# A fused attention and maxout kernel: the maxima of four quadrants go over a scratch row in DRAM instead of a selection product

## The chip, the cores and the metric

The kernel runs on one core of a Trainium2 chip. The metric is the device time of one execution in microseconds; the kernel before took 822.51 us (median of 3 runs, 822.45 to 826.05). A difference of about 0.5% is what a measurement of this kernel can tell from none.

Engines, as the profile names them: PE is TensorE's matmul, PEld its weight load, DVE VectorE, ACT ScalarE, POOL GpSimd, SP the sync engine, which here issues nearly all DMAs from one queue, in order (SPq).

## What is computed

Shapes: x is 4 x 12544 x 128 in float32, 32 inducing vectors of 128, weights 128 x 768 (three of them) and 768 x 128.

```python
def mab(q, kv):
    s = scale * (q @ kv.transpose(0, 2, 1))
    s = s - s.max(-1, keepdims=True)
    a = np.exp(s)
    a /= a.sum(-1, keepdims=True) + 1e-09
    return a @ kv
h = mab(I, x)              # 32 inducing vectors attend over 12544 tokens
x = mab(x, h)              # 12544 tokens attend over 32 states
h = np.maximum(np.maximum(x @ w1, x @ w2), x @ w3)
return h @ w_out
```

The first `mab` is called the first attention here, the second the second attention.

## The kernel before

**Tiling.** The 98 token tiles of a batch (128 tokens each) form seven groups: group 0 has 2 tiles, groups 1 to 6 have 16 each. A full group gives four chunks of 512 columns, group 0 one of 256: 25 chunks a batch, 100 in all. A chunk has six steps j, one for each 128 rows of the hidden width, so there are 600 **slots**.

**One slot** (`advance` and `stage2`): PE makes a product `pu` (line 669) for the next slot into one of two alternating banks and `pv` (675) for this one into another pair; ACT takes the relu of `pu` to `ru` (684); DVE takes the maximum of `pv` and `ru` to `h` (702); ACT rounds `h` to `hi` (691); POOL, or DVE at a few fixed steps, makes the remainder `lo` (699, 705). Six slots later PE adds three products with `hi` and `lo` to `acc` (727 to 729). At the end of a chunk ACT copies `acc` to `o` (744) and SP writes it out (745). Since the `pu` and `pv` banks alternate, a product waits until `ru` or `h` of two slots earlier has been read.

**Windows.** The 24 slots in which the four chunks of a full group g of batch b run are called window g of batch b here; slot numbers below count from the window's first slot (`s0` in the code). In the same window other work is interleaved by hand: the softmax of the second attention for group g + 1 of batch b (`scores_steps`: an exponential, a small sum, `ph` and `pl`), and in batches 0 to 2 the first attention of batch n = b + 1. Window 1 handles groups 0 and 1 of batch n, windows 2 and 3 the groups 2 and 3, window 4 the groups 4 and 5, window 5 group 6. So the first attention of batch 1 runs during batch 0, and so on; that of batch 0 runs before all slots, with code of its own. The matrix products of this work stand in a **burst** at slot 2, and in some windows another at slot 15.

**The order** of every engine is fixed by the program (`manual_schedule`): `plan[s]` holds the steps that `at(s, ...)` and `softmax1`, `softmax2` put into slot s, and `main` runs them after that slot's `advance`.

**A group of the first attention** (`softmax1`). The scores of 32 inducing vectors lie in 128 partitions as four quadrants, each with a quarter of the group's tokens. `attend_max` (line 292) reduces each partition to its negative maximum `mq`. The maximum of a vector is then the least of four partitions, 32 apart:

- `attend_column` (299): ACT multiplies a 128 x 4 mask `quad` by `mq`, giving `md`.
- `attend_spread` (306): PE multiplies `md` by the selection matrix `sel`, so that all 128 partitions hold the four values of their vector in PSUM; in float32 this is two passes, each with a weight load.
- `attend_least` (312, 315, 316): DVE reduces the four values and, from the second group on, takes the least with the running value of the group before.
- `attend_weights` (322): ACT makes the exponential `a` with that value as bias; `attend_scale` (365) makes the factor `al` for the earlier sums; `attend_transpose` (336) transposes `a` on DVE, and `attend_sums` (346) multiplies it with the tokens in a later burst.

The first steps stand at slots s + 2 and s + 3, the others at s + 6 to s + 10, with `LATE` = 12 more slots in windows 2 and 3 (s is 2 or 15).

**Loads.** `load_channels` fetches the transposed tokens xT (1 MB, line 111), `load_tokens` the tokens xg (1 MB, line 100), both on SP's queue, as are the `pT` copies (four per chunk, line 654, from `ph` and `pl`), which are issued two chunks ahead at the fifth slot of each chunk.

Of the kernel before, what the change touches and what calls it, by code (L numbers as in the profile page):

```python
# [8 lines left out]
F32 = mybir.dt.float32  # L9
# [4 lines left out]
ALU = mybir.AluOpType  # L14
AX = mybir.AxisListType
# [10 lines left out]
def kernel(ctx, tc, x, xt, ind_t, w1, w2, w3, w_out, out):  # L26
    nc = tc.nc
    B, N, C = x.shape
    M = ind_t.shape[1]
    DF = w1.shape[1]  # L30
    P = 128
    NT = N // P
    NJ = DF // P
    NQ = P // M
# [18 lines left out]
    ORDER = "a a a a b a a b 0 c d m b a b a b a p d b 1 c s b b b s S m b q 2 c s 3 c s d s s d s"  # L53
    STEPS2 = (3, 5, 7, 8, 9, 10, 11, 13, 14, 15)
    scale = 1.0 / float(C) ** 0.5
    LATE = 12
    LOWVEC = (23, 0, 15, 18)
    LOWLAST = (23, 0, 9, 15, 18)
    UW = 2 * DF + C
# [5 lines left out]
    while t0 < NT:  # L65
        nt = NT % GT if t0 == 0 and NT % GT else GT
        assert nt == GT or nt <= NQ
        g = dict(t0=t0, nt=nt, at=t0 * P)
        groups.append(g)
        t0 += nt  # L70
    NG = len(groups)

    const = ctx.enter_context(tc.tile_pool(name="const", bufs=1))
# [3 lines left out]
    bp = ctx.enter_context(tc.tile_pool(name="bp", bufs=2))  # L77
    hp = ctx.enter_context(tc.tile_pool(name="hp"))
    op = ctx.enter_context(tc.tile_pool(name="op", bufs=2))
    ps = ctx.enter_context(tc.tile_pool(name="ps", bufs=1, space=PSUM))  # L80


# [155 lines left out]
    state = {}  # L238

    def start_batch(b):  # L240
        st = state[b] = {"xT": {}, "xg": {}, "a": {}, "s": {}}
        st["mneg"] = bp.tile([P, NG], F32, name="mneg", tag="mneg")
        st["lst"] = bp.tile([P, NG], F32, name="lst", tag="lst")
        if b == 0:
            st["hg"] = const.tile([P, NG, C], F32, name="hg")
        else:
            st["hs"] = bp.tile([P, C], F32, name="hs", tag="hs")
# [60 lines left out]
    def attend_least(b, gi):  # L308
        st = state[b]
        new, mp = st["mneg"][:, gi : gi + 1], st["mp"]  # L310
        if b == 0 or gi == 0:
            nc.vector.tensor_reduce(out=new, in_=mp[:, :NQ], axis=AX.X, op=ALU.min)
        else:

            nc.vector.tensor_reduce(out=mp[:, NQ : NQ + 1], in_=mp[:, :NQ], axis=AX.X, op=ALU.min)
            nc.vector.tensor_tensor(out=new, in0=mp[:, NQ : NQ + 1], in1=st["mneg"][:, gi - 1 : gi], op=ALU.min)

    def attend_weights(b, gi):
        w = groups[gi]["nt"] * M
        st = state[b]  # L320
        a = wk.tile([P, 512], F32, name="a", tag="a")
        nc.scalar.activation(
            out=a[:, :w],
            in_=st["a"][gi][:, :w],
            func=AF.Exp,
            bias=st["mneg"][:, gi : gi + 1],
            accum_out=st["lst"][:, gi : gi + 1],
        )
        st["a"][gi] = a
# [32 lines left out]
    def attend_scale(b, gi):  # L362
        st = state[b]
        st["al"] = wk.tile([P, 1], F32, name="al", tag="al")
        nc.scalar.activation(
            out=st["al"],
            in_=st["mneg"][:, gi - 1 : gi],
            func=AF.Exp,
            bias=st["mneg"][:, gi : gi + 1],
            scale=-1.0,  # L370
        )

# [397 lines left out]
    def at(s, f, *args):  # L770
        plan[s].append((f, args))
# [13 lines left out]
    def softmax1(b, gi, s, wait=0):  # L785

        at(s + 2, attend_max, b, gi)
        at(s + 3, attend_column, b)
        at(s + 6 + wait, attend_spread, b)
        at(s + 7 + wait, attend_least, b, gi)  # L790
        at(s + 8 + wait, attend_weights, b, gi)
        if gi > 0:
            at(s + 9 + wait, attend_scale, b, gi)
        at(s + 10 + wait, attend_transpose, b, gi)
# [6 lines left out]
    for b in range(B):  # L801
        base = b * per_batch + short
        n = b + 1
        for g in range(1, NG):
# [11 lines left out]
            if n < B:  # L816

                if g == 1:
                    if n == 1:
                        at(s0 + 1, load_tokens, 1, 4)  # L820
                    at(s0 + 4, load_channels, n, 2)
                    first.append((attend_products, n, 0, bank_a[1]))
                    softmax1(n, 0, s0 + 2)
                    second += [(attend_products, n, 1, bank_a[1]), (attend_sums, n, 0)]
                    at(s0 + 16, attend_add, n, 0)
                    softmax1(n, 1, s0 + 15)
                    at(s0 + 16, load_tokens, n + 1, 0)
                    at(s0 + 20, load_channels, n, 3)
                elif g < NG - 2:
                    first += [(attend_products, n, g, bank_a[1]), (attend_sums, n, g - 1)]  # L830
                    at(s0 + 3, attend_add, n, g - 1)
                    softmax1(n, g, s0 + 2, 0 if g == NG - 3 else LATE)
                    at(s0 + 4, load_channels, n, g + 2)
                    more = g + 3
                    if more < NG:
                        at(s0 + 5, load_tokens, n, more)
                    else:
                        at(s0 + 5, load_tokens, n + 1, more - NG + 1)
                    if g == NG - 3:
                        second += [(attend_products, n, g + 1, bank_a[1]), (attend_sums, n, g)]  # L840
                        at(s0 + 16, attend_add, n, g)
                        softmax1(n, g + 1, s0 + 15)
                        at(s0 + 16, load_tokens, n + 1, 2)
                elif g == NG - 2:
                    first += [(attend_products, n, g + 1, bank_a[1]), (attend_sums, n, g)]
                    at(s0 + 3, attend_add, n, g)
                    softmax1(n, g + 1, s0 + 2)
                    at(s0 + 5, load_tokens, n + 1, 3)
                    second.append((attend_sums, n, g + 1))
                    at(s0 + 16, load_tokens, n + 1, 4)  # L850
                    at(s0 + 16, attend_add, n, g + 1)
                    at(s0 + 18, add_quadrants, ("state", n), bank_a[1])
                    at(s0 + 18, total_sums, ("state", n), bank_a[0])
                    at(s0 + 19, invert_total, ("state", n))
                    at(s0 + 19, combine_states, ("state", n), 1)
                    at(s0 + 21, combine_products, ("state", n), bank_a[0])
                    at(s0 + 22, combine_high, ("state", n))
                    at(s0 + 23, combine_low, ("state", n))
                    for r in range(NQ):
                        at(s0 + 25 + 3 * r, combine_rows, ("state", n), r)  # L860
                else:
                    first += [(scores_products, n, 1, bank_a[0]), (scores_products, n, 0, bank_a[1])]
                    softmax2(n, 1, *(s0 + i for i in STEPS2))
                    softmax2(n, 0, *(s0 + i for i in (4, 6, 8, 9, 10, 11, 12, 13, 14, 15)))
                    if n + 1 < B:
                        at(s0 + 18, start_batch, n + 1)
                        at(s0 + 18, load_channels, n + 1, 0)
                        at(s0 + 18, load_channels, n + 1, 1)
# [119 lines left out]
```

## Time and profile before

| What | Before |
|---|---|
| median of 3 runs | 822.51 us |
| span of the profiled execution | 821.3 us |
| median less this span | 1.2 us |
| granted TensorE clock | full in all 40 slices of the page |
| busy: PE, ACT, POOL, DVE | 98%, 91%, 79%, 76% |
| HBM read, written | 48.12 MB, 25.69 MB |
| windows 2, 3 of batch 1 (from the first product of one to that of the next) | 31.3 us each |
| windows 4, 5 of batch 1 | 33.7 and 34.2 us |
| window 2 of batch 3, without a first attention | 28.2 us |

The profile is of one execution. Rows of the timeline give the start, the duration, the engine, the line, the operation, what it writes and reads (output<-inputs) and its shape; in square brackets stands the idle time of the engine just before, and who ended it. A row of the waits gives who waited for whom, the total in us, how often, and the longest. Rows of DMA issues give the tiles, how many, their size and the median time in us from issue to landing; where three numbers stand, they are the least, the median and the greatest. Matmul records overlap: on PE the distance between two starts is what counts.

### The profile page before, as it was taken

What the parts mean: (1) busy time and instruction counts of PE and PEld (TensorE: products, weight loads), DVE (VectorE), ACT (ScalarE), POOL (GpSimd) and SP (SyncE); (2) the same over time, 40 slices, a digit from 0 to 9 for tenths busy, and PEclk for the clock granted to TensorE, in tenths of its full rate; (3) what the DMA queues carried; (4) which work ended last, traced back from release to release, by engine and by line L of the source; (5) the groups of instructions that cost most, each with busy time, mean ns of one, the idle gap of its engine ahead of it and who ended that gap; (6) DMA issues with size and microseconds to landing.
All of it is one profiled execution on the core that took longest, in us unless ns stands there. A gap on an engine that the chain in (4) does not pass through costs nothing.

```text
span 821.3 us, 14725 instructions
## 1 busy us (share of the span) xinstructions
PE 809.0 (98%) x4604; PEld 634.0 (77%) x4604; DVE 627.4 (76%) x1090; ACT 743.5 (91%) x1558; POOL 650.1 (79%) x521
## 2 busy tenths in 40 slices
PE   7989999999999999999999999999999999999998
PEld 5757778778788787777778777877778788787886
DVE  4977778777787687787786877877778788778864
ACT  5779889898899898898999988989889899899996
POOL 1269779778799697787888977977879889888887
PEclk9999999999999999999999999999999999999999
DMA  8844534433443544344334352431223222222221
GB/s 325 310 137 151 188 88 161 161 120 107 136 139 121 154 154 162 84 162 159 110 106 142 116 205 83 159 119 58 63 80 89 71 78 77 65 81 76 63 78 52
DMA packets 44206, 102.51 MB, mean 125 GB/s; under 512 B 9568, under 2 KB 13536, under 8 KB 38880
## 3 DMA queue, kind: packets, MB, share of 16 engines
q1 hardware_dynamic: 43984, 101.44, 38.5%
q8 instruction: 37, 0.61, 0.3%
q14 instruction: 41, 0.34, 0.1%
q10 hardware_dynamic: 144, 0.13, 0.0%
HBM read 48.12 MB, written 25.69 MB: 90 GB/s over the span
## 4 chain that ended last, share of the span: by engine, by line
PE 95%; DMA 2%; DVE 1%; SPq 1%; ACT 1%; issue 0%; ACTq 0%; DVEq 0%
PE acc L727 17%; PE pv L675 16%; PE acc L728 16%; PE acc L729 16%; PE pu L669 16%; PE aux L585 3%; PE acc L726 3%; PE acc L346 3%; PE aux L282 2%; DMA xg<-in_x_dram 2%; PE acc L306 0%; PE pu L272 0%; SPq L100 0%; PE pv L272 0%; PE aux L551 0%; DMA pT<-pl 0%
## 5 line engine op out<-in xcount | busy, mean ns | idle before, releaser
L699 POOL TENSOR_TENSOR lo<-h,hi 128x512 fp32r<-128x512 f32 (+1 forms) x502 | 634.9, 1295 | 129.8 <-ACT hi L691 84.0
L702 DVE TENSOR_TENSOR h<-pv,ru 128x512 f32<-128x512 f32 (+1 forms) x600 | 404.2, 675 | 167.8 <-PE pv L675 81.2
L684 ACT ACTIVATE ru<-pu 128x512 f32<-128x512 f32 (+1 forms) x600 | 375.3, 626 | 52.6 <-PE pu L669 49.7
L691 ACT CAST hi<-h 128x512 fp32r<-128x512 f32 (+1 forms) x600 | 386.4, 644 | 0.4 <-DVE h L702 0.3
L727 PE MATMUL acc<-hi,wo_hi 128*128 128x512 f32 (+1 forms) x600 | 236.9, 395 | 0.0
L675 PE MATMUL pv<-pT,us 128*128 128x512 f32 (+1 forms) x600 | 232.1, 387 | 0.3 <-DVE h L702 0.3
L669 PE MATMUL pu<-pT,us 128*128 128x512 f32 (+1 forms) x600 | 231.5, 386 | 0.4 <-DMA pT<-pl 0.4
L728 PE MATMUL acc<-hi,wo_lo 128*128 128x512 f32 (+1 forms) x600 | 231.5, 386 | 0.0
L729 PE MATMUL acc<-lo,wo_hi 128*128 128x512 f32 (+1 forms) x600 | 231.2, 385 | 0.0
L727 PEld LDWEIGHTS acc<-hi,wo_hi 128*128 128x128 f32 x600 | 112.7, 188 | 30.0 <-issue 8.7
L675 PEld LDWEIGHTS pv<-pT,us 128*128 128x128 f32 x600 | 112.6, 188 | 24.2 <-DVE h L702 1.6
L669 PEld LDWEIGHTS pu<-pT,us 128*128 128x128 f32 x600 | 112.6, 188 | 23.9 <-DMA pT<-pl 0.6
L729 PEld LDWEIGHTS acc<-lo,wo_hi 128*128 128x128 f32 x600 | 112.7, 188 | 23.0
L728 PEld LDWEIGHTS acc<-hi,wo_lo 128*128 128x128 f32 x600 | 112.8, 188 | 21.1
L705 DVE TENSOR_TENSOR lo<-h,hi 128x512 fp32r<-128x512 f32 x98 | 71.3, 727 | 0.7 <-ACT hi L691 0.7
L744 ACT COPY o<-acc 128x512 f32<-128x512 f32 (+1 forms) x99 | 61.1, 617 | 0.0
L726 PE MATMUL acc<-pT,us 128*128 128x512 f32 (+1 forms) x100 | 38.7, 387 | 0.0
L346 PEld LDWEIGHTS acc<-xg,aT 128*32 128x32 f32 x768 | 21.1, 110 | 11.4 <-issue 6.8
L282 PE MATMUL aux<-xT,iT 128*32 128x512 f32 x192 | 25.3, 598 | 1.6 <-ACT xT L274 1.6
L346 PE MATMUL acc<-xg,aT 128*32 128x128 f32 x768 | 25.6, 274 | 0.0
L585 PE MATMUL aux<-xT,hT 128*32 128x512 f32 x192 | 25.1, 603 | 0.0
L192 POOL TENSOR_TENSOR rest<-rest,t 128x768 f32<-128x768 f32 x3 | 5.5, 1824 | 24.3 <-DVE rest L184 24.3
(119 smaller groups left out, 445.4 us busy)
## 6 DMA issues: line engine op xcount, KB each, us to landing
out_dram<-o SPq DMA_DIRECT2D x95, 256.0 KB, 2.0
xg<-in_x_dram SPq DMA_DIRECT2D x23, 1024.0 KB, 6.9
xT<-in_xt_dram SPq DMA_DIRECT2D x18, 1024.0 KB, 5.2
pT<-ph SPq DMA_DIRECT2D x192, 64.0 KB, 2.0
pT<-pl SPq DMA_DIRECT2D x192, 64.0 KB, 2.0
raw<-in_w_dram SPq DMA_DIRECT2D x3, 768.0 KB, 9.5
us<-uh SPq DMA_DIRECT2D x24, 52.0 KB, 1.9
us<-ul SPq DMA_DIRECT2D x24, 52.0 KB, 1.9
```

Source lines behind the costliest of these rows:

```text
L346: nc.tensor.matmul(out=hps[q * M : (q + 1) * M, :C], lhsT=aT[:, t * M : (t + 1) * M], rhs=xg[:, t, :], start=(t < NQ), stop=(t + NQ >= nt),)
L669: nc.tensor.matmul(out=pu[:, :w], lhsT=state[c.b]["us"][:, 2 * j * P : (2 * j + 1) * P], rhs=c.pT[:, :w], start=True, stop=True)
L675: nc.tensor.matmul(out=pv[:, : d.w], lhsT=state[d.b]["us"][:, (2 * j + 1) * P : (2 * j + 2) * P], rhs=d.pT[:, : d.w], start=True, stop=True,)
L684: nc.scalar.activation(out=ru[:, :w], in_=pu[:, :w], func=AF.Relu)
L691: nc.scalar.copy(out=hi[:, : c.w], in_=h[:, : c.w])
L699: nc.gpsimd.tensor_sub(**args)
L702: nc.vector.tensor_max(out=h[:, : d.w], in0=pv[:, : d.w], in1=relus.pop(s)[:, : d.w])
L705: nc.vector.tensor_sub(**low)
L726: nc.tensor.matmul(out=c.acc[:, :w], lhsT=us[:, 2 * DF :], rhs=c.pT[:, :w], start=True, stop=False)
L727: nc.tensor.matmul(out=c.acc[:, :w], lhsT=wo_hi[:, j, :], rhs=c.hh[j][:, :w], start=False, stop=False)
L728: nc.tensor.matmul(out=c.acc[:, :w], lhsT=wo_lo[:, j, :], rhs=c.hh[j][:, :w], start=False, stop=False)
L729: nc.tensor.matmul(out=c.acc[:, :w], lhsT=wo_hi[:, j, :], rhs=c.hl[j][:, :w], start=False, stop=(j == NJ - 1))
```

## The change

For batches 1 to 3 `attend_column`, `attend_spread` and `attend_least` are no longer used. Instead SP writes `mq` (128 values of 4 bytes) to a scratch row in DRAM, ordered so that the four values of a vector lie next to each other, and three slots later reads them back to all 128 partitions, four values each (128 pieces of 16 bytes, `mx`). The tile `mx` has a fifth column, in which the running least of the group before stands, so one DVE reduction over five values (`running_least`) takes the place of two operations. The reduction stands one slot later than `attend_least` stood, and so does `a`; `al` and the transpose stay where they were. `LATE` goes from 12 to 4. The big loads that stood near the transfers move five slots later (one of them two). Batch 0 keeps the product.

```diff
-    LATE = 12
+    LATE = 4
...
+    dp = ctx.enter_context(tc.tile_pool(name="dp", bufs=2, space=bass.MemoryType.DRAM))
...
-        st["mneg"] = bp.tile([P, NG], F32, name="mneg", tag="mneg")
+        if b == 0:
+            st["mneg"] = const.tile([P, NG], F32, name="mneg")
+        else:
+            st["mx"] = bp.tile([P, NG + 1, NQ + 1], F32, name="mx5", tag="mx5")
...
+    def maxima_out(b):
+        st = state[b]
+        row = st["row"] = dp.tile([1, P], F32, name="row", tag="row", bufs=2)
+        nc.sync.dma_start(out=bass.AP(row.tensor, row.offset, [[1, NQ], [NQ, M], [1, 1]]), in_=st["mq"])
+
+    def maxima_in(b, gi):
+        row = state[b]["row"]
+        nc.sync.dma_start(
+            out=state[b]["mx"][:, gi, :NQ], in_=bass.AP(row.tensor, row.offset, [[0, NQ], [NQ, M], [1, NQ]])
+        )
+
+    def running_least(b, gi):
+        st = state[b]
+        nc.vector.tensor_reduce(
+            out=least(st, gi), in_=st["mx"][:, gi, : NQ + (gi > 0)], axis=AX.X, op=ALU.min
+        )
+
+    def least(st, gi):
+        return st["mx"][:, gi + 1, NQ : NQ + 1] if "mx" in st else st["mneg"][:, gi : gi + 1]
...
         at(s + 2, attend_max, b, gi)
-        at(s + 3, attend_column, b)
-        at(s + 6 + wait, attend_spread, b)
-        at(s + 7 + wait, attend_least, b, gi)
-        at(s + 8 + wait, attend_weights, b, gi)
+        at(s + 2, maxima_out, b)
+        at(s + 5, maxima_in, b, gi)
+        at(s + 8 + wait, running_least, b, gi)
+        at(s + 9 + wait, attend_weights, b, gi)
         if gi > 0:
             at(s + 9 + wait, attend_scale, b, gi)
         at(s + 10 + wait, attend_transpose, b, gi)
...
-                    at(s0 + 4, load_channels, n, 2)
+                    at(s0 + 9, load_channels, n, 2)
...
-                    at(s0 + 16, load_tokens, n + 1, 0)
-                    at(s0 + 20, load_channels, n, 3)
+                    at(s0 + 21, load_tokens, n + 1, 0)
+                    at(s0 + 22, load_channels, n, 3)
...
-                    at(s0 + 4, load_channels, n, g + 2)
+                    at(s0 + 9, load_channels, n, g + 2)
...
-                        at(s0 + 5, load_tokens, n, more)
+                        at(s0 + 10, load_tokens, n, more)
...
-                        at(s0 + 16, load_tokens, n + 1, 2)
+                        at(s0 + 21, load_tokens, n + 1, 2)
...
-                    at(s0 + 5, load_tokens, n + 1, 3)
+                    at(s0 + 10, load_tokens, n + 1, 3)
```

Two places show what this does to the order. The first is ACT in window 2 of batch 1, from slot 14 on. Before, `ph` of the second attention stood here without the first attention near it:

```order
L631 CAST ph<-aux_79 128x512
L684 ACTIVATE ru<-pu_81 128x512
L691 CAST hi<-h 128x512
L684 ACTIVATE ru<-pu_82 128x512
L691 CAST hi<-h 128x512
L684 ACTIVATE ru<-pu_81 128x512
```

and the exponential and the factor came at the window's end:

```order
L322 ACTIVATE a,lst<-aux_80,mneg 128x512
L684 ACTIVATE ru<-pu_81 128x512
L691 CAST hi<-h 128x512
L365 ACTIVATE al<-mneg 128x1
L684 ACTIVATE ru<-pu_82 128x512
```

Now both stand one `ru` behind `ph` (the lines are numbered some twenty higher):

```order
L652 CAST ph<-aux_81 128x512
L705 ACTIVATE ru<-pu_83 128x512
L712 CAST hi<-h 128x512
L343 ACTIVATE a,lst<-aux_82,mx_3142 128x512
L386 ACTIVATE al<-mx_3142 128x1
L705 ACTIVATE ru<-pu_84 128x512
```

`a` and `al` have moved up by seven and eight slots, and one `ru` of the stretch between `ph` and the window's end now stands behind them.

The second place is SP's queue in the same window. Before, the two big loads came ahead of the chunk's `out`:

```order
L745 DMA out_dram<-o 128x512
L654 DMA pT<-ph 32x512 x2
L654 DMA pT<-pl 32x512 x2
L111 DMA xT<-in_xt_dram 128x2048
L100 DMA xg<-in_x_dram 128x2048
L745 DMA out_dram<-o 128x512
L654 DMA pT<-ph 32x512 x2
```

Now `row` stands in their place, `mx` behind the `out`, and the loads after both, with the next chunk's `pT` between them:

```order
L766 DMA out_dram<-o 128x512
L675 DMA pT<-ph 32x512 x2
L675 DMA pT<-pl 32x512 x2
L321 DMA row<-mq 4x32x1
L766 DMA out_dram<-o 128x512
L326 DMA mx_3142<-row 128x1x4
L112 DMA xT<-in_xt_dram 128x2048
L675 DMA pT<-ph 32x512 x2
L675 DMA pT<-pl 32x512 x2
L101 DMA xg<-in_x_dram 128x2048
```

So two small transfers have come in, each waiting for the step before it, and the loads have moved past an `out` and, for xg, past four `pT`.

More of the change, by code (lines that the diff above doesn't have):

```diff
@@ L310, in attend_least @@
         new, mp = st["mneg"][:, gi : gi + 1], st["mp"]
[L311 to L316, printed above, removed]
+        nc.vector.tensor_reduce(out=new, in_=mp[:, :NQ], axis=AX.X, op=ALU.min)
+    def maxima_out(b):
[14 more added lines that the diff above has]
+        return st["mx"][:, gi + 1, NQ : NQ + 1] if "mx" in st else st["mneg"][:, gi : gi + 1]
     def attend_weights(b, gi):
@@ L325, in attend_weights @@
             func=AF.Exp,
-            bias=st["mneg"][:, gi : gi + 1],
+            bias=least(st, gi),
             accum_out=st["lst"][:, gi : gi + 1],
@@ L366, in attend_scale @@
             out=st["al"],
-            in_=st["mneg"][:, gi - 1 : gi],
+            in_=least(st, gi - 1),
             func=AF.Exp,
-            bias=st["mneg"][:, gi : gi + 1],
+            bias=least(st, gi),
             scale=-1.0,
@@ L832 @@
                     softmax1(n, g, s0 + 2, 0 if g == NG - 3 else LATE)
-                    at(s0 + 4, load_channels, n, g + 2)
+                    at(s0 + 9, load_channels, n, g + 2)
                     more = g + 3
                     if more < NG:
-                        at(s0 + 5, load_tokens, n, more)
+                        at(s0 + 10, load_tokens, n, more)
                     else:
-                        at(s0 + 5, load_tokens, n + 1, more - NG + 1)
+                        at(s0 + 10, load_tokens, n + 1, more - NG + 1)
                     if g == NG - 3:
```

## The prediction

> **What bounds the kernel now.** I read the page's busy line first, then its chain, then the waits.
>
> ```profile
> span 821.3 us, 14725 instructions
> PE 809.0 (98%) x4604; PEld 634.0 (77%) x4604; DVE 627.4 (76%) x1090; ACT 743.5 (91%) x1558; POOL 650.1 (79%) x521
> PE 95%; DMA 2%; DVE 1%; SPq 1%; ACT 1%; issue 0%; ACTq 0%; DVEq 0%
> PEld pv L675 <- DVE h L702: 1.6, 6, 0.5
> SPq L745 <- ACT o L744: 325.9, 80, 6.6
> ```
>
> TensorE (PE) is the path: 95% of the chain. Matmul records overlap, so 98% busy alone proves little, but the largest wait of the main stretch for another engine is 1.6 us in six pieces. The sync queue (SPq) has room: it stood 325.9 us waiting for `o`. ScalarE (ACT), at 91%, is next in line. So time comes off where PE issues less, and stays off only while ACT and DVE keep up.
>
> **Part 1: the removed product.** The slice below is from window 2 of batch 1. L669 opens each slot.
>
> ```profile
> 304.59 0.39 PE L669 MATMUL pu<-pT,us 128*128 128x512 f32 x1
> 305.72 0.39 PE L669 MATMUL pu<-pT,us 128*128 128x512 f32 x1
> ...
> 306.18 0.28 PE L306 MATMUL acc<-md,sel 128*128 128x4 f32 x2
> ...
> 307.09 0.40 PE L669 MATMUL pu<-pT,us 128*128 128x512 f32 x1
> ...
> 308.23 0.39 PE L669 MATMUL pu<-pT,us 128*128 128x512 f32 x1
> ```
>
> A slot without the product takes 305.72 - 304.59 = 1.13 us. The slot with it and the one behind take 308.23 - 305.72 = 2.51 us; two plain ones would take 2.26, so one spread product costs about 0.25 us of PE. Its two passes of 4 columns are short, but two weight loads stand among others that PE overlaps only in part.
>
> ```profile
> L306 PE MATMUL acc<-md,sel 128*128 128x4 f32 x56 | 8.4, 221 | 0.7 <-ACT md L299 0.6
> ```
>
> 56 passes are 28 products, seven per batch. Batch 0 keeps its seven; 21 go. 21 x 0.25 = **5.2 us less PE work** (5.0 if the rounded pieces are 0.24), all on the path.
>
> The same edit takes 21 `md` from ACT and one small DVE operation in 18 places. These are off the path: DVE has idle time before most `h`, and `md` gives ACT 0.20 us (289.47 to 289.67 below) before its crowded stretch.
>
> **Part 2: the weights move in windows 2 and 3.** With LATE 12 the exponential `a` and `al` stood at slot 22 and 23 of the window, just ahead of the next burst on PE, in which ACT catches up. With LATE 4 both stand at slot 15, right behind `ph`, where ACT is furthest behind.
>
> ```profile
> 289.17 0.39 PE L669 MATMUL pu<-pT,us 128*128 128x512 f32 x1
> 289.47 0.30 ACT L299 ACTIVATE md<-quad,mq 128x4 f32<-128x4 f32 x1
> 289.67 0.59 ACT L684 ACTIVATE ru<-pu 128x512 f32<-128x512 f32 x1
> ...
> 300.30 0.69 ACT L631 CAST ph<-aux 128x512 fp32r<-128x512 f32 x1
> 300.78 0.70 ACT L684 ACTIVATE ru<-pu 128x512 f32<-128x512 f32 x1
> 301.26 0.72 ACT L691 CAST hi<-h 128x512 fp32r<-128x512 f32 x1
> 301.77 0.71 ACT L684 ACTIVATE ru<-pu 128x512 f32<-128x512 f32 x1
> ...
> 303.23 0.39 PE L669 MATMUL pu<-pT,us 128*128 128x512 f32 x1
> ...
> 309.66 0.69 ACT L322 ACTIVATE a<-aux,mneg 128x512 f32<-128x512 f32 x1
> 310.34 0.60 ACT L684 ACTIVATE ru<-pu 128x512 f32<-128x512 f32 x1
> ...
> 311.32 0.31 ACT L365 ACTIVATE al<-mneg 128x1 f32<-128x1 f32 x1
> 311.52 0.60 ACT L684 ACTIVATE ru<-pu 128x512 f32<-128x512 f32 x1
> ```
>
> `a` with its accumulator read holds ACT for 310.34 - 309.66 = 0.68 us, `al` for 0.20: together 0.88. They go in front of the `ru` that began at 301.77 and ended at 302.48. The pu banks alternate, so that `ru` has to be done before the L669 at 303.23: 0.75 us to spare. Without `md`, the `ru` of 289.67 could start as its product ends (289.17 + 0.39 = 289.56, plus some 0.04 of handover), 0.07 earlier, and ACT runs without a gap from there on. 0.75 + 0.07 - 0.88 = -0.06; with the same 0.04 of handover PE waits **0.1 us, six times** (two windows in three batches): **0.6 us back**. Bounds: nothing, if ACT gains elsewhere; the whole 0.88 x 6 = 5.3 us, if the spare time is not there. I take 0.6, worked out from the rows of that very place.
>
> In windows 4 and 5 `a` moves by one slot only, and PE arrives 0.25 us earlier at the tightest point:
>
> ```profile
> 361.84 0.68 ACT L684 ACTIVATE ru<-pu 128x512 f32<-128x512 f32 x1
> 362.77 0.39 PE L669 MATMUL pu<-pT,us 128*128 128x512 f32 x1
> ```
>
> Here the `ru` ends at 362.52, 0.25 ahead of its L669. Minus 0.25, plus the 0.07 of `md`, leaves 0.07: nothing to pay, or 0.04 of handover at six places if it does not hold.
>
> **Part 3: the two transfers.** The trace has no transfer of 4-byte pieces; the nearest rows bound it. The clock starts when `mq` is reduced.
>
> ```profile
> 288.52 0.68 DVE L292 TENSOR_REDUCE mq<-aux 128x1 f32<-128x512 f32 x1
> ...
> 290.66 0.60 ACT L744 COPY o<-acc 128x512 f32<-128x512 f32 x1
> ...
> 291.28 0.34 SPq L745 DMA_DIRECT2D out_dram<-o  x1
> ...
> 294.76 0.68 DVE L702 TENSOR_TENSOR h<-pv,ru 128x512 f32<-128x512 f32 x1
> 295.82 0.69 DVE L702 TENSOR_TENSOR h<-pv,ru 128x512 f32<-128x512 f32 x1 [0.38 <-ACT hi L691]
> ...
> 297.79 0.39 PE L675 MATMUL pv<-pT,us 128*128 128x512 f32 x1
> ```
> ```profile
> out_dram<-o SPq DMA_DIRECT2D x95, 256.0 KB, 2.0
> xg<-in_x_dram SPq DMA_DIRECT2D x23, 1024.0 KB, 6.9
> xT<-in_xt_dram SPq DMA_DIRECT2D x18, 1024.0 KB, 5.2
> pT<-pl SPq DMA_DIRECT2D x192, 64.0 KB, 2.0
> iT<-in_ind_t_dram SPq DMA_DIRECT2D x1, 16.0 KB, 1.8
> ```
>
> `mq` is done at 289.20. `row` goes out and lands at about 291.2 by the 2.0 of a write to DRAM; the `out` between waits for `o` until 291.26 and issues; `mx` issues near 291.7 and lands at 293.7. The reduction that waits stands behind the tenth slot's `h`, and would start at about 295.4. **The pair has 6.2 us and needs some 4.5**, so it costs nothing, bounded below by 3.6 (two at the 1.8 of the smallest) and above by the worst landings of the next rows:
>
> ```profile
> DMA to landing us min/median/max: 1.7/2.0/4.2
> DMA to landing us min/median/max: 1.9/2.0/6.2
> ```
>
> Those are `out` and `pT`, slow where a big load fills the rings; the other edit sends the big loads behind `mx`. In windows 2 and 3 the reduction stands four slots later still, so 15 places are exposed. A late pair stops DVE in order: `h` behind it, then the pv bank that PE writes two slots on. The `h` at 295.82 ends at 296.51 and the L675 that needs its bank is at 297.79, so 1.3 us of lateness is covered.
>
> The Trainium skill speaks against this part: "DMA: Bandwidth & Descriptors", in "Latency and other measured facts", puts an HBM access at 0.2 us on average but 2 us under high load, with the receipt of the write as most of a transfer's fixed cost. The 2.0 median of `out`, a write to DRAM beside running traffic, agrees with the light case; its 4.2 maximum looks like the other. By the high figure each hop would take near 4 us, an estimate from that page, and the second rival below would follow.
>
> **Part 4: queue and loads.** SP issues 42 more transfers at 0.34 us (an `out`) to about 0.6. Queued behind a `row` that waits for `mq` are `out`, `mx`, the big xT load and four `pT`. These `pT` went out at 291.7 and now go near 293, behind 5.2 us of xT, so landing near 298.5. Their chunk starts at slot 18, near 302: covered. The loads are needed 17 slots (19 us) later at the earliest and land in 5 to 7. Both zero, at most a few tenths.
>
> **Sum.** 821.3 - 5.2 + 0.6 = 816.7 us of span, -4.6. The median of the runs, 822.51, is 1.2 above this span, for what lies around it; 822.51 - 4.6 = **817.9 us**, -0.56%.
>
> **Rivals.**
> *ScalarE gives back more.* Its 91% and the negative spare time of windows 2 and 3 speak for it; the 0.75 us rows against. At half of 0.88, six times 0.44 gives 2.6 back, plus 0.2 in windows 4 and 5: 822.51 - 5.2 + 2.8 = 820.1. At the full 5.3 nothing is left: 822.6.
> *The pair lands late (the slower side).* One mechanism: DVE stands at the new reduction until `mx` lands, at 15 places. PE pays from 6.2 + 1.3 = 7.5 us on, 3.7 per transfer. To be slower by 0.5% the 15 places must cost 4.6 + 4.1 = 8.7 us, 0.58 each: 8.1 for the pair, about 4.05 each, near the 4.2 maximum of `out`; then 826.6 and up. For it: pieces of 4 and 16 bytes, 128 to a transfer, and a DRAM round trip, none measured here. Against it: all small transfers at 1.8 to 2.0, and quiet rings.
> *PE's gap is no gain*, because ACT is the true limit: then only ACT's own 21 x 0.20 = 4.2 us comes off, 818.3. The 1.6 us of waits speaks against it.
>
> **How the numbers follow.** Forecast (ends 816.8 to 818.7, from 0 to 1.4 us given back and a few tenths of rounding): 0.58. ScalarE gives back more, 818.7 to 822: 0.23. No gain on PE: 0.05. Pair late, 819 to 826: 0.06; beyond: 0.06. Still faster than the forecast: 0.02. Less than 0.5% (4.1 us, below 818.4) is about what a measurement of this kernel cannot tell from no change. The forecast lies 0.5 us inside that bound, so a fifth of its chance falls on "same": faster 0.46 + 0.05 + 0.02 = 0.53, same 0.40, slower 0.07. The range 816.8 to 820.8 holds the forecast and the near half of the first rival.
>
> **What would show it.** L306 only in the first 120 us or so; slots of 1.13 us where 1.37 stood; window 2 shorter by 0.25 less about 0.1; PE waits on `ru` at slot 19 of windows 2 and 3, and hardly any elsewhere. `row` and `mx` landing at about 2 us each, and no DVE wait for `mx`. The prediction falls if DVE waits for `mx` or if PE waits for `ru` by more than 0.2 us at a place.

## The result, and the profile after

The changed kernel took **1008.92 us** (median of 4 runs, 1004.60 to 1010.26) against 823.81 us for the kernel before on the same chip: a ratio of 1.2237 [1.2199, 1.2276]. It is 22% slower; the forecast, and its range, are far off. The lines of the page that answer to those of before:

```profile
span 1008.2 us, 14734 instructions
PE 861.8 (85%) x4562; PEld 656.6 (65%) x4562; DVE 625.7 (62%) x1072; ACT 748.5 (74%) x1537; POOL 656.5 (65%) x521
PEclk9998988977899888987789978898889999999999
PE 66%; DMA 25%; ACT 3%; DVE 2%; issue 2%; SPq 1%; ACTq 0%; DVEq 0%
```

PE is still the largest share of the chain, but a quarter is now DMA, and the granted clock is below full in most slices up to the 30th. Soon after that the last first attention ends, and the slices are full again. The waits of the same kernel (who waited for whom, total us, how often, longest) name the places; the last row is the sync queue's own:

```profile
DVE mx L332 <- DMA mx<-row: 132.7, 21, 9.7
PE pv L696 <- DVE h L723: 93.9, 18, 8.1
PE pu L690 <- ACT ru L705: 36.8, 11, 5.5
ACT o L765 <- DMA out_dram<-o: 40.5, 13, 4.6
ACT ph L652 <- DMA pT<-ph: 21.1, 4, 5.5
SPq L326 <- DMA row<-mq: 136.8, 21, 8.9
```

All 21 reductions wait for `mx`, not a few, and behind them PE waits for `h`. `mx` in its turn is issued late: SP stands 136.8 us at it until `row` has landed. ScalarE waits for two transfers that have nothing to do with the maxima, `out` and `pT`. The sync queue's rows show the two transfers, at the second group of window 1 and at window 2 of batch 1 (the windows of the prediction):

```profile
347.10 0.59 SPq L321 DMA_DIRECT2D row<-mq  x1
347.79 0.41 SPq L766 DMA_DIRECT2D out_dram<-o  x1
355.72 0.58 SPq L326 DMA_DIRECT2D mx<-row  x1
...
370.08 0.59 SPq L321 DMA_DIRECT2D row<-mq  x1
372.06 0.35 SPq L766 DMA_DIRECT2D out_dram<-o  x1
378.32 0.58 SPq L326 DMA_DIRECT2D mx<-row  x1
```

From the issue of `row` to that of `mx` pass 8.62 and 8.24 us, where the prediction had about 2.5. The reductions behind them, on DVE:

```profile
359.75 0.16 DVE L332 TENSOR_REDUCE mx<-mx 128x1 f32<-128x5 f32 x1 [6.90 <-DMA mx<-row]
...
385.62 0.16 DVE L332 TENSOR_REDUCE mx<-mx 128x1 f32<-128x5 f32 x1 [2.47 <-DMA mx<-row]
```

They start 12.65 and 15.54 us after their `row`. The second wait is the shorter one only because DVE itself had come late by then; ScalarE's rows of that stretch and one of PE's tell why:

```profile
381.28 0.58 ACT L765 COPY o<-acc 128x512 f32<-128x512 f32 x1 [2.51 <-DMA out_dram<-o]
388.75 0.58 ACT L652 CAST ph<-aux 128x512 fp32r<-128x512 f32 x1 [4.87 <-DMA pT<-ph]
```
```profile
389.89 0.80 PE L690 MATMUL pu<-pT,us 128*128 128x512 f32 x1 [4.91 <-ACT ru L705]
```

The `out` issued at 372.06, two microseconds behind `row`, has not landed 9 us later, and `o` stands until 381.28. Then `ph` stands 4.87 us for a `pT` issued behind `mx`, and PE stands 4.91 us for the `ru` behind `ph`. When it restarts, one product takes 0.80 us instead of 0.39. The table of stretches shows the clock (us of each engine's work, the granted clock, the DMA share, GB/s):

```profile
380.00:388.00 8.00, 3.39 (x14) 2.17 (x12) 1.97 (x4) 2.60 (x5) 3.34 (x3) 1.00 0.82 241
388.00:396.00 8.00, 6.11 (x15) 4.82 (x16) 4.11 (x7) 6.53 (x15) 3.47 (x3) 0.57 0.45 144
```

PE works 3.39 of the 8 us from 380 on, and in the next 8 us the granted clock is 0.57. Over the whole span it is 0.919 on average: the 8.1% that are missing are worth 82 us of full clock, part of it while PE stood anyway. The Trainium skill has this rule ("TensorE: Matmul & The Clock Gate", "Part 1: The HAM clock gate": after an idle window of about 3.4 us TensorE runs at half rate until it has been busy again for such a window); the trace agrees here, with a stop of 4.91 us and 0.57 behind it. The prediction didn't price it.

### The profile page after: what moved, and what is told of

The parts are those of the page before. It is cut to its first block, busy times and chain, and to the rows that moved or that the text cites. A ratio compares the mean times of both kernels' runs of the same rounds, so it can differ in the third digit from the quotient of the medians.

```text
span 1008.2 us, 14734 instructions
## 1 busy us (share of the span) xinstructions
PE 861.8 (85%) x4562; PEld 656.6 (65%) x4562; DVE 625.7 (62%) x1072; ACT 748.5 (74%) x1537; POOL 656.5 (65%) x521
## 4 chain that ended last, share of the span: by engine, by line
PE 66%; DMA 25%; ACT 3%; DVE 2%; issue 2%; SPq 1%; ACTq 0%; DVEq 0%
DMA row<-mq 13%; PE pv L696 12%; PE acc L748 11%; PE pu L690 11%; PE acc L749 11%; PE acc L750 11%; DMA mx<-row 8%; PE aux L606 3%; PE aux L286 2%; PE acc L367 2%; DMA pT<-ph 2%; DMA xg<-in_x_dram 2%; PE acc L747 2%; ACT ru L705 2%; DVE h L723 1%
## 5 line engine op out<-in xcount | busy, mean ns | idle before, releaser
L705 ACT ACTIVATE ru<-pu 128x512 f32<-128x512 f32 (+1 forms) x600 | 364.5, 607 | 94.4 <-PE pu L690 90.6
L712 ACT CAST hi<-h 128x512 fp32r<-128x512 f32 (+1 forms) x600 | 375.2, 625 | 2.0 <-DVE h L723 1.9
L696 PE MATMUL pv<-pT,us 128*128 128x512 f32 (+1 forms) x600 | 245.9, 410 | 93.9 <-DVE h L723 93.9
L690 PE MATMUL pu<-pT,us 128*128 128x512 f32 (+1 forms) x600 | 241.2, 402 | 41.4 <-ACT ru L705 36.8
L749 PE MATMUL acc<-hi,wo_lo 128*128 128x512 f32 (+1 forms) x600 | 238.5, 397 | 0.0
L750 PE MATMUL acc<-lo,wo_hi 128*128 128x512 f32 (+1 forms) x600 | 238.3, 397 | 0.0
L696 PEld LDWEIGHTS pv<-pT,us 128*128 128x128 f32 x600 | 119.0, 198 | 125.7 <-DVE h L723 102.4
L765 ACT COPY o<-acc 128x512 f32<-128x512 f32 (+1 forms) x99 | 58.9, 595 | 40.6 <-DMA out_dram<-o 40.5
L332 DVE TENSOR_REDUCE mx<-mx 128x1 f32<-128x5 f32 (+1 forms) x21 | 3.3, 158 | 132.7 <-DMA mx<-row 132.7
L343 ACT ACTIVATE a<-aux,mx 128x512 f32<-128x512 f32 (+1 forms) x21 | 13.4, 638 | 72.0 <-DVE mx L332 72.0
L652 ACT CAST ph<-aux 128x512 fp32r<-128x512 f32 x24 | 14.7, 612 | 26.4 <-DMA pT<-ph 21.1
```

What stands on the lines that cost most here:

```text
L690: nc.tensor.matmul(out=pu[:, :w], lhsT=state[c.b]["us"][:, 2 * j * P : (2 * j + 1) * P], rhs=c.pT[:, :w], start=True, stop=True)
L696: nc.tensor.matmul(out=pv[:, : d.w], lhsT=state[d.b]["us"][:, (2 * j + 1) * P : (2 * j + 2) * P], rhs=d.pT[:, : d.w], start=True, stop=True,)
L705: nc.scalar.activation(out=ru[:, :w], in_=pu[:, :w], func=AF.Relu)
L712: nc.scalar.copy(out=hi[:, : c.w], in_=h[:, : c.w])
L749: nc.tensor.matmul(out=c.acc[:, :w], lhsT=wo_lo[:, j, :], rhs=c.hh[j][:, :w], start=False, stop=False)
L750: nc.tensor.matmul(out=c.acc[:, :w], lhsT=wo_hi[:, j, :], rhs=c.hl[j][:, :w], start=False, stop=(j == NJ - 1))
```

## The experiments

Each kernel differs from the one named in the lines shown. "Before" in a ratio is the kernel before, run on the same chip between them.

**First question: are the parts without the transfers as predicted?** In e1 `mq` goes straight into `mx` and the transfers are left out, so each partition uses its own quadrant's maximum.

```diff
-        mq = wk.tile([P, 1], F32, name="mq", tag="mq")
+        mq = wk.tile([P, 1], F32, name="mq", tag="mq") if b == 0 else st["mx"][:, gi, :1]
...
-        at(s + 2, maxima_out, b)
-        at(s + 5, maxima_in, b, gi)
```

> Leaves out: the exchange between quadrants (batches 1 to 3 use each quadrant's own maximum); no product, no row, no mx, all else as changed. The theory that the whole loss hangs on the two transfers, and that the terms for PE (-5.2 us) and ScalarE (+0.6 us) were right: 817 to 819 us, 0.5 to 0.6% below before, PE at full clock, PE waits for ru under 2 us in all. The rival, that LATE 4 and the moved loads do harm of their own: over 823 us.

820.03 us (median of 8), ratio 0.9961 [0.9946, 0.9975], span 817.7. So the whole loss is in the two transfers: 1008.2 - 817.7 = 190.5 us of span. The forecast of 816.7 for the span was 1.0 too low. The rows of PE in window 2 of batch 1, slots 18 and 19, show where most of it comes from. The first row is of the kernel before, the others are e1's:

```profile
302.09 0.39 PE L669 MATMUL pu<-pT,us 128*128 128x512 f32 x1
...
299.46 0.39 PE L690 MATMUL pu<-pT,us 128*128 128x512 f32 x1
300.69 0.50 PE L690 MATMUL pu<-pT,us 128*128 128x512 f32 x1
302.19 0.39 PE L690 MATMUL pu<-pT,us 128*128 128x512 f32 x1
```

The two slots take 1.23 and 1.50 us; the same two took 1.14 and 1.36 before (302.09, then 303.23 and 304.59 in the prediction's rows). So the stop is at the slot that the prediction named, but costs 0.23 us instead of 0.1.

In e2 the product stays: the kernel before with LATE 4 and the moved loads.

```diff
-    LATE = 12
+    LATE = 4
...
-                    at(s0 + 4, load_channels, n, 2)
+                    at(s0 + 9, load_channels, n, 2)
...
```

> The product as before, with LATE 4 and the loads five slots later: the other half of the change alone. If the loss hangs on the transfers: 822 to 825 us (ScalarE's 0.88 us in windows 2 and 3 gives back at most 1.4 us). If the moved loads or the moved exponential are what costs: over 830 us.

840.04 us (5 runs), ratio 1.0215 [1.0192, 1.0239]: slower, by a mechanism that neither theory had.

```profile
PE acc L306 <- ACT o L744: 10.3, 6, 1.7
```

With LATE 4 the product in windows 2 and 3 comes eight slots earlier, into a spare `acc` bank that `o` is still copying out, and PE stands for it six times, 10.3 us of the 14.9 by which the span of 836.2 us is longer. Behind two of these stops the granted clock fell as well, to 0.50 from 303 to 306 us, and products took up to 0.63 us. The stop ahead of that lasted 1.71 us, so here less than the 3.4 us of the rule above was enough; behind the other four the clock stayed full. LATE 4 is cheap only without the product, so the two edits aren't independent.

**Second question: why does `row` take 8 us?** It ran on four of the sixteen transfer engines. In e3 its 128 values lie in the order of the partitions, which sixteen engines write, each eight neighbours; in e4 the four engines stay, but every vector's four values get a line of 512 bytes to themselves.

```diff
e3
-        nc.sync.dma_start(out=bass.AP(row.tensor, row.offset, [[1, NQ], [NQ, M], [1, 1]]), in_=st["mq"])
+        nc.sync.dma_start(out=bass.AP(row.tensor, row.offset, [[1, P], [1, 1]]), in_=st["mq"])
e4
-        row = st["row"] = dp.tile([1, P], F32, name="row", tag="row", bufs=2)
+        row = st["row"] = dp.tile([1, P * M], F32, name="row", tag="row", bufs=2)
...
-        nc.sync.dma_start(out=bass.AP(row.tensor, row.offset, [[1, NQ], [NQ, M], [1, 1]]), in_=st["mq"])
+        nc.sync.dma_start(out=bass.AP(row.tensor, row.offset, [[1, NQ], [P, M], [1, 1]]), in_=st["mq"])
```

(e4 reads `mx` by the same pattern; in e3 `mx` takes four neighbouring partitions' values in place of a vector's four quadrants)

> The row is written in the order of the partitions, [[1,128]], the same 128 pieces of 4 bytes; the shift that a vector gets is then another one, which cancels. The packets of the trace put the changed row on 4 engines (4 of 16 completion packets); now 16 can take it. If the row takes 8 us because only 4 engines carry it, 32 pieces each: it lands in 2 to 3.5 us and the time falls below 930 us. If 4-byte writes into one 512-byte stretch of DRAM are taken one after the other at their destination: it still takes 7 to 9 us and the time stays within 980 to 1020 us.

> The four values of a vector still side by side, but each vector in a 512-byte line of its own (32 lines); still 4 engines and 128 pieces. If neighbouring writes wait for each other at the destination: the row lands in 2 to 4 us, time below 930 us. If the engines or the count of pieces set the time: 7 to 9 us as before, time 980 to 1020 us.

e3: 987.14 us (2 runs), ratio 1.1989 [1.1960, 1.2018]; SP waits for `row` nearly as long as in the change. e4: **820.47 us** (8 runs), ratio 0.9969 [0.9957, 0.9981]: the loss is gone. The number of engines isn't the cause; the place of the values is. SP's wait for `row` in e3, the same in e4, and SP's rows in e4 (window 2 of batch 1):

```profile
SPq L326 <- DMA row<-mq: 128.9, 21, 8.2
```
```profile
SPq L326 <- DMA row<-mq: 5.1, 6, 1.1
```
```profile
289.65 0.59 SPq L321 DMA_DIRECT2D row<-mq  x1
291.64 0.35 SPq L766 DMA_DIRECT2D out_dram<-o  x1
292.08 0.58 SPq L326 DMA_DIRECT2D mx<-row  x1
```

In e4 `mx` goes out 2.43 us behind `row`, as soon as the `out` between them has gone, and no reduction waits.

**Third question: how near may the values be?** e6 gives each vector 64 bytes, e10 gives 32; the change gave 16, e4 512.

```diff
e6
-        row = st["row"] = dp.tile([1, P * M], F32, name="row", tag="row", bufs=2)
-        nc.sync.dma_start(out=bass.AP(row.tensor, row.offset, [[1, NQ], [P, M], [1, 1]]), in_=st["mq"])
+        row = st["row"] = dp.tile([1, 16 * M], F32, name="row", tag="row", bufs=2)
+        nc.sync.dma_start(out=bass.AP(row.tensor, row.offset, [[1, NQ], [16, M], [1, 1]]), in_=st["mq"])
```

(e10: 8 in place of 16)

> The kernel of e4 with 64 bytes in place of 512 from one vector's values to the next: a row of 2048 bytes that the same four transfer engines write. Theory A (what waits for one another are writes of 4 bytes that share a stretch of 64 bytes; the change had sixteen of them in such a stretch, here four): `row` is in before `mx` is issued at 2.0 to 2.75 us behind its own issue, as in e4, and the time is 820 to 821 us. Theory B (they share a stretch of 512 bytes; the change had 128 writes in one, e4 four, here 32): `row` to the issue of `mx` is 3 to 5 us, between e4's 2.0 to 2.75 and the change's 8.1 to 10.0, and the time 821 to 840 us.

> The kernel of e4 with 32 bytes from one vector's values to the next, so eight writes of 4 bytes in a stretch of 64 bytes (the change has sixteen, e6 four), and each of the four engines writes twice in succession into each stretch (the change: four times, e6: once). Theory A (an engine's second write into its stretch waits): slower than e6 by an amount that grows with the repeats: the change's 8.1 to 10.0 us for `row` stand for three repeats in each of eight stretches, some 0.25 to 0.3 us for each repeat, so one repeat in each of sixteen stretches gives 16 x 0.25 to 0.3 = 4 to 5 us more than e6's 2.4, `row` to the issue of `mx` 6 to 7 us, and the time over 850 us. Theory B (only a stretch that holds more writes than some number is slow, or stretches of 32 bytes are what counts): 2.0 to 2.8 us and 820 to 821 us.

e6: 820.07 us (9 runs), ratio 0.9973 [0.9962, 0.9983], as e4. e10: 827.14 us (8 runs), ratio 1.0050 [1.0038, 1.0063]: between, where neither theory had put it (A had said 6 to 7 us for `row`). SP's waits for `row` in e6 and in e10, and in e10 the reduction's:

```profile
SPq L326 <- DMA row<-mq: 7.5, 6, 2.0
```
```profile
SPq L326 <- DMA row<-mq: 35.5, 21, 4.0
DVE mx L332 <- DMA mx<-row: 15.7, 15, 2.1
```

With 64 bytes SP waits at six places, with 32 at all 21, 1.7 us on average, with 16 (the change) 6.5 us. So the time doesn't go with the count of repeats as theory A had it; it sets in between 64 and 32 bytes and rises steeply. The Trainium skill ("DMA: Bandwidth & Descriptors", "Specifications") says that below 512 bytes a DMA engine reads, modifies and writes; that fits writes which wait for the one before them at the same place. How large that place is, these runs don't show. From issue to issue `mx` is 8.1 to 10.0 us behind `row` in the change and 3.4 to 5.1 in e10, where any stretch holds half as many writes. Halved once more, as in e6, that would be no more than the 2.0 to 2.75 us that e4 needs with 512 bytes. So a shared place of 64 bytes and one of 512 would both give these times, and since the row grows with the spacing (512, 1024 and 2048 bytes in all), its whole length could be what counts.

**Fourth question: is it the writes alone, and what does a slow `row` do to others?** In e7 `row` is written as in the change, but `mx` is read from a row of zeros that was written once at the start, in lines of 512 bytes, so nobody reads `row`. In e8 `row` is written as in e4, and `mx` is read from 512 bytes of zeros packed as in the change.

```diff
e7 (e8: the same line, with the patterns exchanged)
-        row = state[b]["row"]
+        row = still[0]
...
-            out=state[b]["mx"][:, gi, :NQ], in_=bass.AP(row.tensor, row.offset, [[0, NQ], [NQ, M], [1, NQ]])
+            out=state[b]["mx"][:, gi, :NQ], in_=bass.AP(row.tensor, row.offset, [[0, NQ], [P, M], [1, NQ]])
```

> The kernel of the change, with `row` written as there (128 writes of 4 bytes in 512 bytes), but `mx` is read from a row of zeros in DRAM that is written once at the start, in lines of 512 bytes: nothing waits for the slow `row` any more. (The other quadrants' maxima are zeros, and the shift of the exponent is then another one, which cancels.) Theory A (only the wait for `row` and what stands behind it in SP's queue costs time): 820 to 822 us. Theory B (the slow `row` also holds back the transfers that are issued behind it on the same queue, the output `out` of the chunk above all, which ScalarE's `o` waits for): `out` lands later than its 2.4 us of e4 by some us, `o` waits for it, and the time is over 830 us.

> The kernel of e4 for `row`, but `mx` is read from a row of zeros of 512 bytes that is written once at the start, its 128 values next to each other as in the change; nothing waits for `row`. (The shift is another one, which cancels.) Theory A (reads of 4 values from neighbouring places are as quick as from lines of their own; the 3.3 to 7.2 us of `mx` in the change came from the unfinished writes and the loads behind it): `mx` is in 1.5 to 2.5 us after its issue, and the time is 820 to 821 us. Theory B (reads within 512 bytes wait for one another as the writes do): `mx` takes 3.3 us or more from its issue, seen in the reduction that waits for it or in the completions, and the time is 821 to 840 us.

e8: 820.47 us (5 runs), ratio 0.9973 [0.9955, 0.9990]; no reduction waits: packed reads are quick. e7: 934.33 us (2 runs), ratio 1.1355 [1.1312, 1.1399]. A `row` that nobody reads still costs 928.2 - 817.7 = 110.5 us of span. In e7's timeline (second group of window 4, batch 0):

```profile
195.54 0.59 SPq L323 DMA_DIRECT2D row<-mq  x1
196.22 0.42 SPq L772 DMA_DIRECT2D out_dram<-o  x1
196.69 0.58 SPq L328 DMA_DIRECT2D mx<-still  x1
...
207.43 0.16 DVE L334 TENSOR_REDUCE mx<-mx 128x1 f32<-128x5 f32 x1 [6.15 <-DMA mx<-still]
```

`mx` needs nothing from `row` and is issued 1.15 us behind it, and yet the reduction gets it 10.7 us after its issue. Not all of the 110.5 us is such late landing, though. SP itself stands for the unread `row` before it issues an `out`, and for 24.2 and 7.0 us more before `xg` and `xT`:

```profile
SPq L772 <- DMA row<-mq: 29.1, 8, 5.1
```

In the trace the transfers take turns at eight completion semaphores (the counters that tell of a landing), so the eighth transfer behind a `row` waits until that `row` has landed. This is how the program is built. The `out` and `mx` in the rows above are the first and second behind `row`, and are late all the same.

Is it the queue's order? In e11 ScalarE issues that unread `row`, on a queue of its own. In e9 the row of e7 is ordered so that sixteen engines write eight values each, every one into another stretch of 64 bytes.

```diff
e11
-        nc.sync.dma_start(out=bass.AP(row.tensor, row.offset, [[1, NQ], [NQ, M], [1, 1]]), in_=st["mq"])
+        nc.scalar.dma_start(out=bass.AP(row.tensor, row.offset, [[1, NQ], [NQ, M], [1, 1]]), in_=st["mq"])
e9
+        nc.sync.dma_start(out=bass.AP(row.tensor, row.offset, [[1, 16], [16, P // 16], [1, 1]]), in_=st["mq"])
```

> The kernel of e7 with `row` issued by ScalarE in place of SyncE, so on another queue; `mx`, `out`, `pT` and the loads stay on SyncE's. Theory A (a slow `row` holds back what stands behind it in the same queue alone): `mx` and `out` land as in e8, the reduction and `o` wait no more; ScalarE pays for 21 issues and for its wait for the maxima, which the rows of ScalarE will show, some 1 to 2 us at a place, so 821 to 860 us. Theory B (it holds the transfer engines, whatever queue the others come by, or the place in DRAM): the reduction waits for `mx` as in e7 (82 us in 15 places) and the time is 920 us or more.

> The kernel of e7 (`row` in 512 bytes, nobody waits for it, `mx` from a row of zeros; 934 us) with another order of the 128 values in `row`: sixteen transfer engines write eight values each, and each of the eight goes to another stretch of 64 bytes, so that no engine writes twice into one stretch; a stretch still gets sixteen writes, one from each engine. Theory A (an engine's next write into the stretch that it has just written waits for the one before): no such pair is left, what is issued behind `row` lands as in e8, and the time is 820 to 823 us. Theory B (any writes of 4 bytes into one stretch wait for one another, whichever engine sends them): as slow as e7, 900 us or more.

e11: 930.95 us (2 runs), ratio 1.1312 [1.1189, 1.1435], as e7; another queue frees nobody:

```profile
q10 hardware_dynamic: 2916, 0.14, 0.2%
```
```profile
196.24 0.53 ACTq L323 DMA_DIRECT2D row<-mq  x1
...
198.43 0.35 SPq L772 DMA_DIRECT2D out_dram<-o  x1
198.83 0.58 SPq L328 DMA_DIRECT2D mx<-still  x1
207.64 0.16 DVE L334 TENSOR_REDUCE mx<-mx 128x1 f32<-128x5 f32 x1 [4.50 <-DMA mx<-still]
207.65 0.58 ACT L771 COPY o<-acc 128x512 f32<-128x512 f32 x1 [3.20 <-DMA out_dram<-o]
```

The packets of `row` are now on q10 (144 on that queue before; the 2772 more are 132 for each `row`, its 128 values and one completion for each of four engines), `out` and `mx` on SP's, and both still land some 9 us after their issue.

Do the transfer engines move the data late? The table of stretches of the change, around the `row` of 347.10, and ScalarE's row behind the `out` of 347.79:

```profile
348.30:349.50 1.20, 1.20 (x7) 1.00 (x6) 0.74 (x2) 1.20 (x3) 0.58 (x1) 1.00 0.81 226
349.50:357.00 7.50, 5.92 (x27) 4.56 (x25) 2.54 (x4) 4.47 (x9) 5.34 (x4) 1.00 0.01 2
```
```profile
358.64 0.58 ACT L765 COPY o<-acc 128x512 f32<-128x512 f32 x1 [4.57 <-DMA out_dram<-o]
```

In the first stretch the engines move 226 GB/s, some 270 KB, which holds all of `row` and the 256 KB of `out`. In the next 7.5 us they move next to nothing, and yet `out` has landed only at 358.6. So the data were moved early, and what comes late is the end of the writes.

e9: 885.50 and 899.68 us in two runs, beside 823.02 for the kernel before. Quicker than e7, so the order or the number of engines has a part in it, but still far from e8's 820: no engine writes twice into the same 64 bytes here, so if stretches of 64 bytes are what counts, writes of different engines wait for one another too, and theory A falls. With a larger stretch an engine would still meet its own writes, and e9 doesn't decide between the theories.

**Fifth question: what else of the change is worth keeping?** e5 is e4 with LATE 12: without the product nothing keeps the reduction and `a` from going back to the window's end.

```diff
-    LATE = 4
+    LATE = 12
```

> The kernel of e4 (each vector's four values in a line of 512 bytes of its own) with LATE 12 in place of 4: in windows 2 and 3 the two operations for the shift on ScalarE go back to the end of the window. Theory (the stop of PE in windows 2 and 3 comes from these two operations, which stand ahead of `ru`): in the run with the own quadrant's maxima the slots 18 and 19 of these windows lasted 1.235 and 1.49 us in place of 1.133 and 1.36, about 0.23 us a window over six windows; without them 1.4 us come back, so 818.5 to 819.5 us and a ratio of 0.994 to 0.996 with the kernel before. Rival (the stop has another source, or the pair's values come too late for the end of the window as for its start): 820.0 to 821.0, as e4. If the pair is late at this place too, the reduction is seen waiting for `mx` in windows 2 and 3.

**819.18 us** (6 runs), ratio 0.9964 [0.9951, 0.9977], the fastest of all; e4's interval overlaps, so the 1.3 us between the medians rest on the trace. PE's rows at the slots of e1's above:

```profile
299.49 0.39 PE L690 MATMUL pu<-pT,us 128*128 128x512 f32 x1
300.63 0.39 PE L690 MATMUL pu<-pT,us 128*128 128x512 f32 x1
301.99 0.39 PE L690 MATMUL pu<-pT,us 128*128 128x512 f32 x1
```

1.14 and 1.36 us again: the stop is gone, as expected (0.23 x 6 = 1.4 us).

e12 puts e5's big loads back into their old slots.

```diff
-                    at(s0 + 9, load_channels, n, g + 2)
+                    at(s0 + 4, load_channels, n, g + 2)
...
-                        at(s0 + 10, load_tokens, n, more)
+                        at(s0 + 5, load_tokens, n, more)
...
```

> The kernel of e5 (lines of 512 bytes, LATE 12) with the big loads back in the slots that they had before the change: one or two loads of 1024 KB then stand in SyncE's queue between `row` and `mx`, or just ahead of `row`, at most places. Theory A (the move of the loads is needed: `mx` is read behind up to 2048 KB on the same transfer engines, whose loads took 5.2 and 6.9 us to land before the change): the pair takes 4.2 us plus some 5 us at the 15 places without LATE, the reduction runs at 8.5 to 10 us in place of 5.5 to 6.1 from the issue of `row`, PE pays from 7.5 us on, 1 to 2.5 us a place, so 832 to 856 us, and the reduction is seen waiting for `mx`. Theory B (the small transfers are not held up by loads, since four of the sixteen engines carry them between the loads' packets): 818.5 to 820 us, as e5, and the reduction waits at no place.

827.66 us (6 runs), ratio 1.0052 [1.0037, 1.0068], under theory A's 832 but on its side. In the timeline at window 4 of batch 0, and in the waits:

```profile
159.27 0.59 SPq L321 DMA_DIRECT2D row<-mq  x1
...
159.96 0.61 SPq L112 DMA_DIRECT2D xT<-in_xt_dram  x1
160.66 0.38 SPq L101 DMA_DIRECT2D xg<-in_x_dram  x1
...
161.88 0.58 SPq L326 DMA_DIRECT2D mx<-row  x1
169.15 0.16 DVE L332 TENSOR_REDUCE mx<-mx 128x1 f32<-128x5 f32 x1 [3.68 <-DMA mx<-row]
```
```profile
DVE mx L332 <- DMA mx<-row: 13.9, 7, 3.7
```

`row` is in after 2.61 us, but `mx`, behind two loads of 1024 KB, takes until 7.27 us after its own issue. Seven reductions wait, not fifteen: windows 2 and 3 have LATE 12 for cover, and at the other places no load stands between or it is through in time. The move of the loads is worth 827.66 - 819.18 = 8.5 us once `row` is quick (some 7 by the two ratios, since e5 and e12 ran on different chips).

## Why the prediction was wrong

**The step that failed** is Part 3: "The pair has 6.2 us and needs some 4.5", with an upper bound from the worst landings of `out` and `pT`. The pair took 12.65 and 15.54 us in the rows above. The mechanism is one that the bounds couldn't hold: 128 writes of 4 bytes, packed into 512 bytes of DRAM, take 8 us and more to land there, and wait for one another as far as the runs tell. The rows that it was bounded with are transfers whose pieces are long (a row of `out` has 512 values) and lie at places of their own; they say nothing on short pieces that share a place. That the chosen 4.5 us itself was sound for a pair without that sharing, e4 shows: its `mx` goes out 2.43 us behind `row`, and the reduction at 6 us doesn't wait. The prediction named the pieces and the DRAM round trip as unmeasured, yet took every small transfer's 1.8 to 2.0 us as evidence on them. It weighed a rule of the Trainium skill on DRAM under load ("DMA: Bandwidth & Descriptors", "Latency and other measured facts"), which would have given near 4 us a hop; e4 and e8, on the same loaded DRAM, need no such figure. A pair late beyond 826 us had a chance of 0.06.

**The price of lateness was too low as well.** The second rival had the right place and the right wait, but by its price, what exceeds 1.3 us at each reduction, the 132.7 us of waits would cost 132.7 - 21 x 1.3 = 105 us; the span grew by 190.5 over e1's. Three things were left out. (1) Part 4 held that what is queued behind `row` is covered. A slow `row` keeps `out` and `mx` from landing, whatever queue it is on, makes the eighth transfer behind it wait, and sends the `pT` behind `mx` out late; ScalarE waits for `out` (40.5 us) and for `pT` (21.1 us). e7, where nobody reads `row`, shows what a slow `row` does to others to be worth 110.5 us; that `mx` must be issued after `row` has landed adds 1008.2 - 928.2 = 80. (2) "15 places are exposed": all 21 were, since four slots more in windows 2 and 3 don't cover 15 us. (3) Stops of PE bring half clock, 82 us of full clock in all, part of it while PE stood anyway.

**Part 1** was right in kind and near in size: e5, without the product and without the stop, has a span of 817.1, 4.2 us under before, where 5.2 were taken (3.6 by the medians on the same chip, 822.73 and 819.18). L306's successor (L310) ran for batch 0 alone, and the slot of 1.37 us with the product became one of 1.13. Taken window by window from the two traces, a product is worth 0.25 us in windows 1 to 3 and 0.19 in windows 4 and 5, 4.7 in all, and the part ahead of the slots is 0.6 shorter. One place gives 1.1 back: a slot at 561.60 takes 2.25 us in place of 1.13, behind a DVE `lo` that took 1.83 us this once.

**Part 2** had the right slot and the right cause (e1 shows the stop, e5 its end), mis-sized: 0.23 us at a place instead of 0.1, 1.4 in all instead of 0.6. Part of the difference is that the product behind the stop took 0.50 us in place of 0.39.

**Part 4**, that moving the loads costs nothing, holds for the loads themselves; e12 shows that the move is needed, which the prediction only used as a reason in Part 3. With e4's spacing the change as a whole comes out at 820.47 us, inside the range given, in the region of the first rival.

What stays open: why the end of the packed writes comes so late, and by what it keeps other transfers from landing (the engines had moved `row` and the first `out` early); how large the shared place is, or whether the length of the whole row counts (a row of one length with other spacings wasn't tried); how much of e7's 110.5 us is late landing and how much the wait for a completion semaphore; and how much of the 190.5 us is half clock rather than standing.

## What to carry to other kernels

A transfer's cost isn't its byte count: scattering 128 single 4-byte values into 512 bytes of DRAM took 8 us where the same values in groups of four, 64 bytes apart, took little over 2, so give scattered values places of their own and read them back with the pattern. Before bounding an unmeasured transfer by the nearest rows, ask whether those rows share its piece size and its destination's spacing; if not, the bound is a guess and the range has to say so. And price a late transfer by everything that lands behind it and by the clock that a standing TensorE loses, not by its own reader alone.

## What the runs showed of the hardware

That the spacing of 4-byte writes in DRAM, or the extent that grows with it, decides their time: with 512, 64, 32 and 16 bytes from one group of four to the next, SP's wait for 21 such transfers was 5.1, 7.5, 35.5 and 136.8 us, while after packed reads (e8) no reduction waited. That such a write reaches past its own queue: `out`, 256 KB, landed in 2.0 us (median) before the change and some 9 us after its issue behind a packed `row`, in e11 with `row` on another queue. That the engines are done long before: 226 GB/s up to 349.5 us, 2 GB/s for the 7.5 us behind, and the landing at 358.6. And that in e2 two of six stops of TensorE of about 1.7 us were followed by half clock (0.50 from 303 to 306 us).
